# Products with the centroids in four column tiles, and one-hot rows moved by four copies

## The chip, the cores and the metric

The kernel runs on one core of a Trainium2 chip. A core has a matrix engine (TensorE, PE in the rows), a vector engine (VectorE, DVE), a scalar engine (ScalarE, ACT), GpSimd (POOL) and SyncE (SP), which here issues nearly all copies. The metric is device time in microseconds of one execution, lower is better; the time of a kernel is the median of its runs.

## The reference

Clustered attention, and behind it two layers of experts. In the attention a key is seen by a query only where both have the same nearest centroid.

```python
q_n = q / (np.linalg.norm(q, axis=-1, keepdims=True) + 1e-06)        # k_n, c_n likewise
q_assign = np.argmax(np.einsum('bhsd,hcd->bhsc', q_n, c_n), axis=-1)  # k_assign likewise
mask = q_assign[:, :, :, None] == k_assign[:, :, None, :]
scores = np.where(mask, scale * np.matmul(q, k.transpose(0, 1, 3, 2)), -1000000000.0)
attn = softmax(scores)
x = np.matmul(attn, v)      # then _moe_ref(x, ...) and _moe2_ref(x, ...), eight experts each
```

There are 2 x 8 heads of 768 positions and 64 columns, with 16 centroids for each head. All data are float32.

## The kernel before

The attention works on *pairs* of heads, eight of them (`pairs`, 0 to 7). The 128 partitions hold the 64 columns of two heads. For each pair the loop `for i in range(len(seq) + LAG + 1)` makes twelve *turns* (`sl` 0 to 11), one for each of six blocks of 128 queries and each head. In a turn stand, in this order for every engine:

- `scores`: TensorE writes `pss` (one block of queries against all keys) into one of two PSUM buffers. Its operands are two pairs of tiles: `x1`, `y1` (high and low halves of q and k) and `x2`, `y2`, which hold one more half product in partitions 0 to 63 and *one-hot rows* in partitions 64 to 79: the query's centroid, and 0 or -2^100 for the key's. That product is the mask.
- `softmax_max`: DVE takes the maximum, `nm`.
- `tr_p` of the block two turns back: TensorE transposes `pe` into `ppt`, ACT and DVE copy it out as `pt`.
- `attend` and `fin`, in some turns: TensorE's `av` in turns 0, 4, 6 and 10, `px` with the `norm` operations `ri`, `lp` and `x` on DVE in turns 1 and 7.
- one step of `prep` for the *next* pair (step 0 in turn 0, and so on; in pair 0 the steps begin at turn `P0` = 2), and loads of q, k and v for the pair after it (`LD`).
- `softmax_exp`: ACT's `pe`. The scores' PSUM buffer is free for the turn after next when it is done.

`ps_t` is a pool of three PSUM buffers, which `plog`, `plt`, `poh`, `ppt`, `px` and the small `pws` share.

The steps of `prep` work as follows. `part` splits q and k into high and low halves: `qh` and `kh` on ACT, `ql` on DVE, `kl` on POOL. `logits` multiplies q and k with the centroids (`plog`), for the first 384 positions and then for the other 384, and scales by the centroids' norms (`lt`). `logits_t` transposes `lt` (`plt`). `argmax` finds the nearest centroid (`mx`, `eq`; POOL multiplies `eq` by `rev`), `first` makes the one-hot `oh`. `operands` copies the halves into `x1`, `y1`, `x2`, `y2`: twelve copies on SP's queue, six for each head. `oh_t` transposes `oh` (`poh`), writes `ot` on DVE and copies its rows into `x2` and `y2`, each row of 16 partitions, four copies.

Every engine takes its instructions in the program's order, and SP's queue too: a copy that waits for its data holds up those behind it. In pair 6 the weights' pool takes over the memory of the preparation (`prepared.close()`) and the first weight piece is split there (`wh` on ACT, `wl` on DVE). Pairs 3, 4 and 5 carry in addition the routing of the first layer, many small operations on DVE.

Of the kernel before, what the change touches and what calls it, by code (L numbers as in the profile page):

```python
# [15 lines left out]
BIG = float(2.0 ** 100)  # L16
WARM = 8
P0 = 2
LD = {7: "q", 8: "k", 9: "v"}
WARM2 = 6  # L20


# [6 lines left out]
def attention(tc, end, ps_t, ident, wu, q, k, v, centroids, wg, x_half, lg_sb, consts, before_half, after_half, extra, slot):  # L29
# [13 lines left out]
    with ExitStack() as ctx:  # L43
# [11 lines left out]
        def cpy(dst, src):  # L55
            nc.sync.dma_start(dst.bitcast(F32), src.bitcast(F32))

        def centroid_norms():

            nc.vector.tensor_tensor(c_sq, cw, cw, op=ALU.mult)  # L60
            p = ps_t.tile([P, 512], F32, tag="t", name="pc")[:64, :NP]
            for hp in range(NP):
                for t in range(2):
                    nc.tensor.matmul(p[32 * t:32 * t + 2 * G, hp:hp + 1], c_sq[:, hp].rearrange("p j g -> p (j g)"),
                                     ones, start=True, stop=True)
            nc.scalar.sqrt(c_n, p)
            nc.vector.tensor_scalar_add(c_n, c_n, 1e-6)
            nc.vector.reciprocal(c_n, c_n)
# [17 lines left out]
        def gate_loads(wgv):  # L86
            for j in range(2):
# [2 lines left out]

        cw = one.tile([P, NP, 2, G], F32, name="cw")
        c_sq = one.tile([P, NP, 2, G], F32, name="c_sq")
        c_n = one.tile([64, NP], F32, name="c_n")
        ones = one.tile([P, 1], F32, name="a_ones")
        rev = one.tile([P, G], F32, name="rev")
        msc = one.tile([64, 2], F32, name="msc")
        rw = end.tile([P, NP, P + 2 * E], F32, name="rw")
        xs = {(nm, s, j): one.tile([P, S], F32R, name=f"{nm}_{s}{j}")
              for s in range(2) for j in range(2) for nm in ("x2", "y2")}

        warm0 = one.tile([1, 1], F32, name="warm0")
        st = {}
# [13 lines left out]
        def part(pi, nm):  # L116

            d = st[pi]
            t = d[nm] = w1.tile([P, S], F32R, tag=nm, name=nm)
            x = d[nm[0]]  # L120
            if nm == "qh":
                nc.scalar.activation(t, x, AF.Copy, scale=scale)
            elif nm == "ql":
                nc.vector.scalar_tensor_tensor(t, x, scale, d["qh"], op0=ALU.mult, op1=ALU.subtract)
            elif nm == "kh":
                nc.scalar.copy(t, x)
            else:
                nc.gpsimd.tensor_tensor(t, x, d["kh"], op=ALU.subtract)
# [15 lines left out]
            cpy(xs["y2", s, j][:D], d["kl"][r])  # L144

        def logits(pi):
            b, hp = pairs[pi]
            d = st[pi]
            d["lt"] = lt = w1.tile([64, S], F32, tag="lt", name="lt")
            for hf in range(2):  # L150
                p = ps_t.tile([P, 512], F32, tag="t", name="plog")[:64, :W]
                for t, nm in enumerate("qk"):
                    nc.tensor.matmul(p[32 * t:32 * t + 2 * G], cw[:, hp].rearrange("p j g -> p (j g)"),  # L153
                                     d[nm][:, hf * W:(hf + 1) * W], start=True, stop=True)
                if hf == 0:
                    nc.scalar.mul(lt[:, :W], p, c_n[:, hp:hp + 1])
                elif pi == 0:
                    nc.scalar.mul(lt[:, W:], p, c_n[:, hp:hp + 1])
                else:
                    nc.vector.tensor_scalar_mul(lt[:, W:], p, c_n[:, hp:hp + 1])  # L160

        def logits_t(pi):
            d = st[pi]
            p = ps_t.tile([P, 512], F32, tag="t", name="plt")[:, :C * 4 * G]
            d["lg"] = p.rearrange("p (c t j g) -> p c t j g", c=C, t=2, j=2)
            for c in range(C):
                nc.tensor.transpose(p[:, c * 4 * G:(c + 1) * 4 * G], d["lt"][:, c * P:(c + 1) * P], ident[:64, :64])
# [18 lines left out]

        def oh_t(pi):
            d = st[pi]
            ot = w1.tile([64, S], F32R, tag="lt", name="ot")
            ohv = d["oh"].rearrange("p (c i) g -> p c (i g)", i=4)  # L190
            for hf in range(2):
                p = ps_t.tile([P, 512], F32, tag="t", name="poh")[:64, :W]
                for c in range(HALF):
                    nc.tensor.transpose(p[:, c * P:(c + 1) * P], ohv[:, hf * HALF + c], ident)
                nc.vector.tensor_scalar(ot[:, hf * W:(hf + 1) * W], p, msc[:, 0:1], msc[:, 1:2],
                                        op0=ALU.mult, op1=ALU.add)
            s = pi % 2
            for j in range(2):
                cpy(xs["x2", s, j][64:64 + G], ot[j * G:(j + 1) * G])
                cpy(xs["y2", s, j][64:64 + G], ot[(2 + j) * G:(3 + j) * G])  # L200

        def first_mask(j):

# [142 lines left out]
        def last():  # L346
# [83 lines left out]
        for i in range(len(seq) + LAG + 1):  # L430
            cur = seq[i] if i < len(seq) else None
            if cur:
                scores(*cur)
                softmax_max(*cur)
            if LAG <= i < len(seq) + LAG:
                pi, c, j = seq[i - LAG]
                tr_p(pi, c, j)
                if j == 1 and c % HALF == HALF - 1:
                    hf = c // HALF
                    for w, at in enumerate(AT_LAST if pi == NPR - 1 else AT):  # L440
                        f = (lambda pi=pi, hf=hf, w=w: attend(pi, hf, w)) if w < 2 else (lambda pi=pi, hf=hf: fin(pi, hf))
                        if w < 2 or pi < NPR - 1 or hf == 0:
                            avq.append((i + at, f))
            while avq and (avq[0][0] <= i or i >= len(seq) + LAG - 1):
                avq.pop(0)[1]()
            if cur:
                pi = cur[0]
                sl = i % n
                if sl in LD:
                    load(pi + 2, LD[sl])  # L450
                if i == 0:
                    for _ in masks[1]:
                        pass
                if i == 1:
                    first_rows(1)
                ps = sl - P0 + (sl - P0 > 6) if pi == 0 else sl
                if pi + 1 < NPR and 0 <= ps < len(prep):
                    prep[ps](pi + 1)
                if pi >= 1 and sl % 2 == 0:
                    next(more, None)  # L460
                softmax_exp(*cur)
                if pi == NPR - 2 and sl == len(prep):
                    prepared.close()
                slot(pi, sl)
            if bg:
                bg.pop(0)()
# [1482 lines left out]
```

## Time and profile before

| | |
|---|---|
| median of 3 runs | 626.52 us (625.83 to 628.45) |
| the profiled execution | 623.46 us, span of its records 621.7 us |
| TensorE (PE) busy | 570.0 us, 92% of the span |
| VectorE (DVE) busy | 466.4 us, 75% |
| ScalarE (ACT) busy | 421.8 us, 68% |
| GpSimd (POOL) busy | 216.4 us, 35% |
| attention part | about 0 to 281 us, the experts from there |

Busy time of the matmul engine is modelled, since matmuls are pipelined; the distance from one instruction's start to the next one's start is the safer number. A timeline row gives the start and the length in us, the engine, the source line, the operation, the tiles (out<-in) and how often it follows itself; in brackets the idle time before it and what ended that.

### The profile page before, as it was taken

The page shows a single profiled execution, that of the slowest core. Times are in us where ns is not written, and L with a number is a line of the kernel's source. Part 1 is how long each engine was busy: PE and PEld are TensorE (multiplying, and loading weights), DVE is VectorE, ACT ScalarE, POOL GpSimd, SP SyncE. Part 2 cuts the span into 40 slices and gives each one's busy share as a digit, 9 for nine tenths or more (in the row PEclk, how much of TensorE's full clock was granted, in tenths as well). Part 3 has the DMA queues.
Part 4 walks back from the last instruction along what each step waited for, and adds up shares of the span by engine and source line. Part 5 has one row for each costly group of instructions (what it writes and reads, how often), then busy time and mean ns, then how long its engine had stood idle before and what let it go on. Part 6 is the DMA issues. An engine that isn't in the chain of part 4 may idle for free.

```text
span 621.7 us, 14524 instructions
## 1 busy us (share of the span) xinstructions
PE 570.0 (92%) x5428; PEld 467.1 (75%) x5428; DVE 466.4 (75%) x1185; ACT 421.8 (68%) x902; POOL 216.4 (35%) x427
## 2 busy tenths in 40 slices
PE   7899999998999998986799999997788999999993
PEld 2676767676767675656778998996777888999993
DVE  4776777677989676867577778789678566979881
ACT  3666666777676667963585687776774566979781
POOL 7702020201341110105743355636523723253541
PEclk9999999999999999999899999999999999999997
DMA  5589654656519891522456856976963677898930
GB/s 138 155 208 289 166 135 118 143 134 134 148 29 224 258 249 23 198 69 105 146 179 236 277 181 206 305 259 191 302 206 98 220 222 240 293 307 291 333 126 23
DMA packets 75518, 117.55 MB, mean 189 GB/s; under 512 B 10504, under 2 KB 43400, under 8 KB 75441
## 3 DMA queue, kind: packets, MB, share of 16 engines
q1 hardware_dynamic: 72017, 106.76, 57.4%
q0 software_dynamic: 3264, 9.72, 4.8%
q8 instruction: 45, 0.74, 0.5%
q14 instruction: 32, 0.26, 0.1%
q10 hardware_dynamic: 160, 0.07, 0.0%
HBM read 84.28 MB, written 12.87 MB: 156 GB/s over the span
## 4 chain that ended last, share of the span: by engine, by line
PE 61%; DVE 15%; ACT 11%; issue 4%; DMA 4%; POOL 2%; SPq 0%; ACTq 0%; DVEq 0%; POOLq 0%
PE ph L949 15%; PE py L1021 13%; PE av L280 9%; PE pss L238 8%; PE ppt L268 6%; PE pz L996 3%; DVE nm L246 3%; DVE wl L846 3%; ACT pe L254 2%; PE pyo L1637 2%; ACT wh L839 2%; ACT pt L270 1%; PE pxt L926 1%; PE plog L153 1%; DMA x2d<-xo 1%
## 5 line engine op out<-in xcount | busy, mean ns | idle before, releaser
L846 DVE SCALAR_TENSOR_TENSOR wl<-raw,sw,wh 128x1024 f16<-128x1024 f32 x128 | 163.6, 1285 | 19.0 <-ACT wh L839 18.8
L839 ACT ACTIVATE wh<-raw,sw 128x1024 f16<-128x1024 f32 x128 | 146.1, 1148 | 3.0 <-DMA x<-ot 2.5
L246 DVE TENSOR_REDUCE nm<-pss 128x1 f32<-128x768 f32 x96 | 91.4, 952 | 41.5 <-PE pss L238 37.8
L254 ACT ACTIVATE pe<-pss,nm 128x768 f32<-128x768 f32 x96 | 87.1, 907 | 24.3 <-DVE nm L246 24.3
L949 PEld LDWEIGHTS <-wh 128*128 128x128 f16 x1152 | 87.7, 99 | 17.4 <-issue 12.8
L238 PE MATMUL pss<-y,x 128*128 128x384 f32 x384 | 95.4, 370 | 4.0 <-ACT pe L254 3.2
L268 PE MATMUL ppt<-ident,pe 128*128 128x128 f32 x576 | 80.5, 275 | 3.3 <-ACT pt L270 1.4
L238 PEld LDWEIGHTS pss<-y,x 128*128 128x128 f32 x384 | 64.7, 194 | 24.6 <-issue 12.5
L270 ACT COPY pt<-ppt 128x384 f32<-128x384 f32 x128 | 57.9, 482 | 29.6 <-PE ppt L268 29.3
L949 PE MATMUL ph<-xh,wh 128*128 128x192 f16 (+14 forms) x576 | 67.3, 240 | 9.9 <-ACT hr L955 4.6
L268 PEld LDWEIGHTS ppt<-ident,pe 128*128 128x128 f32 x576 | 69.2, 142 | 8.9 <-ACT pt L270 2.3
L1021 PEld LDWEIGHTS <-wh 128*128 128x128 f16 x960 | 72.4, 99 | 4.3 <-issue 1.0
L280 PE MATMUL av<-pt,v 128*64 128x384 f32 x384 | 68.8, 494 | 0.0
L949 PE MATMUL ph<-xl,wh 128*128 128x192 f16 (+14 forms) x576 | 67.2, 240 | 0.4 <-DVE xl L928 0.3
L949 PE MATMUL ph<-xh,wl 128*128 128x192 f16 (+14 forms) x576 | 67.3, 240 | 0.0
L951 ACT ACTIVATE hh<-ph 128x128 f16<-128x128 f32 (+14 forms) x144 | 44.6, 316 | 25.9 <-PE ph L949 24.7
L958 DVE SCALAR_TENSOR_TENSOR hl<-ph,hh 128x192 f16<-128x192 f32 (+14 forms) x126 | 40.8, 335 | 26.1 <-ACT hh L951 25.9
L1021 PE MATMUL py<-hh,wh 128*128 128x192 f16 (+13 forms) x480 | 46.6, 239 | 1.5 <-ACT hh L951 1.0
L1021 PE MATMUL py<-hl,wh 128*128 128x192 f16 (+13 forms) x480 | 46.8, 239 | 0.5 <-DVE hl L958 0.2
L949 PEld LDWEIGHTS <-wl 128*128 128x128 f16 x576 | 45.5, 99 | 1.9
L280 PEld LDWEIGHTS av<-pt,v 128*64 128x64 f32 x384 | 24.8, 136 | 28.4 <-issue 28.3
L1021 PE MATMUL py<-hh,wl 128*128 128x192 f16 (+13 forms) x480 | 46.1, 239 | 0.0
(326 smaller groups left out, 873.4 us busy)
## 6 DMA issues: line engine op xcount, KB each, us to landing
raw<-in_moe_w SPq DMA_DIRECT2D x64, 1024.0 KB, 6.2
y<-kh SPq DMA_DIRECT2D x31, 192.0 KB, 4.0
x<-qh SPq DMA_DIRECT2D x30, 192.0 KB, 4.2
q<-in_q SPq DMA_DIRECT2D x8, 384.0 KB, 4.9
k<-in_k SPq DMA_DIRECT2D x8, 384.0 KB, 4.6
x<-ql SPq DMA_DIRECT2D x16, 192.0 KB, 3.5
v<-in_v SPq DMA_DIRECT2D x8, 384.0 KB, 3.3
out<-zt SPq DMA_DIRECT2D x1, 3072.0 KB, 11.3
```

The source lines that it names most:

```text
L238: nc.tensor.matmul(p[:, hf, :W], xx[:, c * P:(c + 1) * P], yy[:, hf * W:(hf + 1) * W], start=a, stop=o)
L246: nc.vector.tensor_reduce(nm, p[:, :, :W], axis=AX.XY, op=ALU.max, negate=True)
L254: nc.scalar.activation(pe, p[:, :, :W], AF.Exp, bias=d["nm", c, j], scale=1.0, accum_out=d["sm"][:, c, j:j + 1])
L268: nc.tensor.transpose(p[:, kc * P:(kc + 1) * P], pe[:, kh, kc * P:(kc + 1) * P], ident)
L270: eng(pt[:, kh * HALF:(kh + 1) * HALF, (c % HALF) * P:(c % HALF + 1) * P], p.rearrange("p (a b) -> p a b", a=HALF))
L280: nc.tensor.matmul(p[j * D:(j + 1) * D, :W], d["v"][:, j, kc, :], d["pt", hf, j][:, kc, :], start=(kc == 0), stop=(kc == C - 1))
L839: nc.scalar.activation(hi[:, :, s], x[:, :, s], AF.Copy, scale=sw)
L846: nc.vector.scalar_tensor_tensor(lo[:, :, s], x[:, :, s], sw, hi[:, :, s], op0=ALU.mult, op1=ALU.subtract, accum_out=fl)
L949: nc.tensor.matmul(p[:, :N], w[:, c, fs], x[:, c, :N], start=(k == 0), stop=(k == 11))
L951: nc.scalar.activation(hh[:, f, :N], p[:, :N], AF.Relu)
L958: nc.vector.scalar_tensor_tensor(hl[:, f, :N], p[:, :N], 0.0, hh[:, f, :N], op0=ALU.max, op1=ALU.subtract)
L1021: nc.tensor.matmul(p[:, :N], w[:, f, s], x[:, f, :N], start=(k == 0), stop=(k == 23))
```

## The change

- `logits` makes one round for both halves of the positions: four products, each with 32 output partitions (0, 32, 64, 96), in one PSUM buffer. `lt` is one tile of 128 partitions and 384 columns, written by one operation (DVE; ACT in pair 0's own).
- `logits_t` and `oh_t` make three transposes of 128x128 instead of six narrower ones.
- `ot` is made twice, once for each head, with the other head's rows scaled to zero (`msc`, which is now made from `own` on DVE and POOL at the start), so that the rows of both heads lie side by side and four copies of 32 partitions move them (before: four copies of 16 partitions, one for each head and each of x and y). `x2` and `y2` of both heads are one tile (`xs2`).
- `prep` has another order: `logits` in turn 0, `logits_t` and `qh` in 1, `argmax`, `kh` and `kl` in 2, `ql` in 3, `first` and `operands` in 4, `oh_t` in 7 (before: `qh` in 0, `ql`, `kh`, `kl` in 1, `logits` in 2, `logits_t` in 3, `argmax` and `operands` in 4, `first` in 5, `oh_t` in 8).
- The loads of q and k stand behind `oh_t` in turn 7, that of v in turn 8 (before: turns 7, 8 and 9). In pair 0 they move with the steps, to turns 9 and 10.

```diff
-LD = {7: "q", 8: "k", 9: "v"}
+LD = {7: "qk", 8: "v"}
...
-            d["lt"] = lt = w1.tile([64, S], F32, tag="lt", name="lt")
+            d["lt"] = lt = w1.tile([P, W], F32, tag="lt", name="lt")
+            p = ps_t.tile([P, 512], F32, tag="t", name="plog")[:, :W]
             for hf in range(2):
-                p = ps_t.tile([P, 512], F32, tag="t", name="plog")[:64, :W]
                 for t, nm in enumerate("qk"):
-                    nc.tensor.matmul(p[32 * t:32 * t + 2 * G], cw[:, hp].rearrange("p j g -> p (j g)"),
+                    r = 64 * hf + 32 * t
+                    nc.tensor.matmul(p[r:r + 2 * G], cw[:, hp].rearrange("p j g -> p (j g)"),
                                      d[nm][:, hf * W:(hf + 1) * W], start=True, stop=True)
-                if hf == 0:
-                    nc.scalar.mul(lt[:, :W], p, c_n[:, hp:hp + 1])
-                elif pi == 0:
-                    nc.scalar.mul(lt[:, W:], p, c_n[:, hp:hp + 1])
-                else:
-                    nc.vector.tensor_scalar_mul(lt[:, W:], p, c_n[:, hp:hp + 1])
+            if pi == 0:
+                nc.scalar.mul(lt, p, c_n[:, hp:hp + 1])
+            else:
+                nc.vector.tensor_scalar_mul(lt, p, c_n[:, hp:hp + 1])
...
-            for c in range(C):
-                nc.tensor.transpose(p[:, c * 4 * G:(c + 1) * 4 * G], d["lt"][:, c * P:(c + 1) * P], ident[:64, :64])
+            for c in range(HALF):
+                nc.tensor.transpose(p[:, c * P:(c + 1) * P], d["lt"][:, c * P:(c + 1) * P], ident)
...
-            ot = w1.tile([64, S], F32R, tag="lt", name="ot")
-            ohv = d["oh"].rearrange("p (c i) g -> p c (i g)", i=4)
+
+            ot = w1.tile([P, 2, W], F32R, tag="ot", name="ot")
+            ohv = d["oh"].rearrange("p (c i) g -> p c (i g)", i=8)
+            p = ps_t.tile([P, 512], F32, tag="t", name="poh")[:, :W]
+            for c in range(HALF):
+                nc.tensor.transpose(p[:, c * P:(c + 1) * P], ohv[:, c], ident)
+            for j in range(2):
+                nc.vector.tensor_scalar(ot[:, j], p, msc[:, j, 0:1], msc[:, j, 1:2], op0=ALU.mult, op1=ALU.add)
+            s = pi % 2
             for hf in range(2):
-                p = ps_t.tile([P, 512], F32, tag="t", name="poh")[:64, :W]
-                for c in range(HALF):
-                    nc.tensor.transpose(p[:, c * P:(c + 1) * P], ohv[:, hf * HALF + c], ident)
-                nc.vector.tensor_scalar(ot[:, hf * W:(hf + 1) * W], p, msc[:, 0:1], msc[:, 1:2],
-                                        op0=ALU.mult, op1=ALU.add)
-            s = pi % 2
-            for j in range(2):
-                cpy(xs["x2", s, j][64:64 + G], ot[j * G:(j + 1) * G])
-                cpy(xs["y2", s, j][64:64 + G], ot[(2 + j) * G:(3 + j) * G])
+                for t, nm in enumerate(("x2", "y2")):
+                    r = 64 * hf + 32 * t
+                    cpy(xs2[nm, s][64:96, :, hf * W:(hf + 1) * W], ot[r:r + 32])
...
         prep = [
-            lambda i: part(i, "qh"),
-            lambda i: (part(i, "ql"), part(i, "kh"), part(i, "kl")),
             lambda i: logits(i),
-            lambda i: logits_t(i),
-            lambda i: (argmax(i), operands(i, 0), operands(i, 1)),
-            lambda i: first(i),
+            lambda i: (logits_t(i), part(i, "qh")),
+            lambda i: (argmax(i), part(i, "kh"), part(i, "kl")),
+            lambda i: part(i, "ql"),
+            lambda i: (first(i), operands(i, 0), operands(i, 1)),
             lambda i: None,
             lambda i: None,
             lambda i: oh_t(i),
...
-                if sl in LD:
-                    load(pi + 2, LD[sl])
...
-                ps = sl - P0 + (sl - P0 > 6) if pi == 0 else sl
+                ps = sl - P0 if pi == 0 else sl
                 if pi + 1 < NPR and 0 <= ps < len(prep):
                     prep[ps](pi + 1)
+                for nm in LD.get(ps, ()):
+                    load(pi + 2, nm)
```

What this does to the order on VectorE in turns 1 to 4 of pair 1, from the `norm` operations' last, `x`, to the one-hot `oh`, was before:

```order
L323 TENSOR_TENSOR x<-px,ri 128x3x128
L124 SCALAR_TENSOR_TENSOR ql<-q,qh 128x768
L246 TENSOR_REDUCE nm<-pss 128x1
L270 COPY pt_762<-ppt 128x3x128
L160 TENSOR_SCALAR lt<-plog,c_n 64x384
L246 TENSOR_REDUCE nm<-pss 128x1
L270 COPY pt_791<-ppt 128x3x128
L246 TENSOR_REDUCE nm<-pss 128x1
L270 COPY pt_762<-ppt 128x3x128
L174 TENSOR_REDUCE mx<-plt 128x24
L176 TENSOR_TENSOR eq<-plt,mx 128x384
L246 TENSOR_REDUCE nm<-pss 128x1
```

The same stretch of VectorE in the changed kernel, with `lt` ahead of it in turn 0:

```order
L325 TENSOR_TENSOR x<-px,ri 128x3x128
L248 TENSOR_REDUCE nm<-pss 128x1
L272 COPY pt_764<-ppt 128x3x128
L175 TENSOR_REDUCE mx<-plt 128x24
L177 TENSOR_TENSOR eq<-plt,mx 128x384
L248 TENSOR_REDUCE nm<-pss 128x1
L272 COPY pt_793<-ppt 128x3x128
L124 SCALAR_TENSOR_TENSOR ql<-q,qh 128x768
L248 TENSOR_REDUCE nm<-pss 128x1
L272 COPY pt_764<-ppt 128x3x128
L184 TENSOR_REDUCE m_832<-eq 128x24
L186 TENSOR_TENSOR oh<-eq,m_832 128x384
```

`mx` and `eq` moved from turn 4 to turn 2, `ql` from turn 1 to turn 3, and the last two rows, `first`, from turn 5 to turn 4.

VectorE again, in turns 7 to 9 of pair 1, around `ot`, before:

```order
L323 TENSOR_TENSOR x<-px,ri 128x3x128
L246 TENSOR_REDUCE nm<-pss 128x1
L270 COPY pt_950<-ppt 128x3x128
L195 TENSOR_SCALAR ot<-poh,msc 64x384 x2
L1386 CAST cap<-cap_i 128x1
```

And in the changed kernel:

```order
L325 TENSOR_TENSOR x<-px,ri 128x3x128
L197 TENSOR_SCALAR ot<-poh,msc 128x384 x2
L248 TENSOR_REDUCE nm<-pss 128x1
L272 COPY pt_955<-ppt 128x3x128
L1395 CAST cap<-cap_i 128x1
```

`ot` moved ahead of turn 8's `nm`.

SyncE's queue at the end of pair 1's preparation of pair 2, from the last operand copy on (`x_` and `y_` with a number are here the tiles `x2` and `y2`), before:

```order
L56 DMA y_01_168<-kl 64x768
L114 DMA q<-in_q 128x768
L114 DMA k<-in_k 128x768
L56 DMA x_00_165<-ot 16x768
L56 DMA y_00_166<-ot 16x768
L56 DMA x_01_167<-ot 16x768
L56 DMA y_01_168<-ot 16x768
```

And in the changed kernel:

```order
L56 DMA y_0_166<-kl 64x768
L56 DMA x_0_165<-ot 32x2x384
L56 DMA y_0_166<-ot 32x2x384
L56 DMA x_0_165<-ot 32x2x384
L56 DMA y_0_166<-ot 32x2x384
L114 DMA q<-in_q 128x768
L114 DMA k<-in_k 128x768
```

The two loads moved behind the four copies.

## Rows read from the trace of the kernel before

**Rows 1.** Timeline of PE, pair 2 (start us, length us).
```profile
81.80 0.90 PE L307 MATMUL px<-rw,avo 128*128 128x144 f32 x6
82.61 0.97 PE L238 MATMUL pss<-y,x 128*128 128x384 f32 x4
...
84.17 0.51 PE L153 MATMUL plog<-q,cw 128*32 128x384 f32 x1
...
85.36 0.51 PE L153 MATMUL plog<-q,cw 128*32 128x384 f32 x1 [0.35 <-ACT pt L270]
...
86.15 0.95 PE L238 MATMUL pss<-y,x 128*128 128x384 f32 x4
...
89.75 2.16 PE L280 MATMUL av<-pt,v 128*64 128x384 f32 x12
...
92.15 0.97 PE L238 MATMUL pss<-y,x 128*128 128x384 f32 x4
...
93.53 0.96 PE L238 MATMUL pss<-y,x 128*128 128x384 f32 x4
...
100.71 0.92 PE L194 MATMUL poh<-ident,oh 128*64 128x128 f32 x6
```

**Rows 2.** Waits, 20 to 285 us (total us, times, longest).
```profile
PE plog L153 <- ACT pt L270: 3.6, 6, 1.4
...
ACT wh L839 <- DMA x<-ot: 2.5, 1, 2.5
...
PE pss L238 <- DMA y<-ot: 0.8, 1, 0.8
```

**Rows 3.** Costliest groups on the page (busy us, mean ns of one).
```profile
L246 DVE TENSOR_REDUCE nm<-pss 128x1 f32<-128x768 f32 x96 | 91.4, 952 | 41.5 <-PE pss L238 37.8
L254 ACT ACTIVATE pe<-pss,nm 128x768 f32<-128x768 f32 x96 | 87.1, 907 | 24.3 <-DVE nm L246 24.3
```

**Rows 4.** Windows: length, then busy us of each engine in pair 5.
```profile
180.00:200.00 20.00, 19.32 (x134) 13.51 (x132) 19.55 (x43) 12.82 (x28) 8.05 (x8) 1.00 0.61 151
```

**Rows 5.** Timeline of PE in the experts' part, four column tiles.
```profile
347.81 0.72 PE L1666 MATMUL pq<-yt,wgc 128*32 128x304 f32 x8
```

**Rows 6.** Timeline of DVE, pair 3.
```profile
122.47 0.55 DVE L174 TENSOR_REDUCE mx<-plt 128x24 f32<-128x384 f32 x1
123.05 0.56 DVE L176 TENSOR_TENSOR eq<-plt,mx 128x384 f32<-128x384 f32 x1
...
129.78 0.96 DVE L246 TENSOR_REDUCE nm<-pss 128x1 f32<-128x768 f32 x1 [1.67 <-PE pss L238]
...
131.86 0.96 DVE L246 TENSOR_REDUCE nm<-pss 128x1 f32<-128x768 f32 x1
...
133.20 1.25 DVE L195 TENSOR_SCALAR ot<-poh,msc 64x384 fp32r<-64x384 f32 x2
```

**Rows 7.** Timeline of ACT, pair 3, turn 1.
```profile
114.23 0.86 ACT L126 CAST kh<-k 128x768 fp32r<-128x768 f32 x1
```

**Rows 8.** Timelines of DVE and POOL: the first masks, and pair 2's argmax.
```profile
13.24 1.65 DVE L217 TENSOR_TENSOR oh<-eq,m 128x192 f32<-128x192 f32 x1
...
20.86 0.36 DVE L217 TENSOR_TENSOR oh<-eq,m 128x192 f32<-128x192 f32 x1
...
12.87 1.79 POOL L128 TENSOR_TENSOR kl<-k,kh 128x768 fp32r<-128x768 f32 x1
...
91.83 0.99 POOL L177 TENSOR_TENSOR eq<-eq,rev 128x384 f32<-128x384 f32 x1 [5.65 <-DVE eq L176]
```

**Rows 9.** Timeline of SP's queue, pair 0.
```profile
29.68 0.55 SPq L56 DMA_DIRECT2D x<-ql  x1
...
36.98 0.60 SPq L56 DMA_DIRECT2D y<-kl  x1
```

**Rows 10.** Copies issued, all of the span (KB each, median us to landing).
```profile
q<-in_q SPq DMA_DIRECT2D x8, 384.0 KB, 4.9
...
x<-ot SPq DMA_DIRECT2D x14, 48.0 KB, 2.3
```

More of the change, by code (lines that the diff above doesn't have):

```diff
@@ L60, in centroid_norms @@
             nc.vector.tensor_tensor(c_sq, cw, cw, op=ALU.mult)
-            p = ps_t.tile([P, 512], F32, tag="t", name="pc")[:64, :NP]
+            p = ps_t.tile([P, 512], F32, tag="t", name="pc")[:, :NP]
             for hp in range(NP):
-                for t in range(2):
+                for t in range(4):
                     nc.tensor.matmul(p[32 * t:32 * t + 2 * G, hp:hp + 1], c_sq[:, hp].rearrange("p j g -> p (j g)"),
@@ L92, in attention @@
         c_sq = one.tile([P, NP, 2, G], F32, name="c_sq")
-        c_n = one.tile([64, NP], F32, name="c_n")
+        c_n = one.tile([P, NP], F32, name="c_n")
         ones = one.tile([P, 1], F32, name="a_ones")
         rev = one.tile([P, G], F32, name="rev")
-        msc = one.tile([64, 2], F32, name="msc")
+        msc = one.tile([P, 2, 2], F32, name="msc")
         rw = end.tile([P, NP, P + 2 * E], F32, name="rw")
-        xs = {(nm, s, j): one.tile([P, S], F32R, name=f"{nm}_{s}{j}")
-              for s in range(2) for j in range(2) for nm in ("x2", "y2")}
+        xs2 = {(nm, s): one.tile([P, 2, S], F32R, name=f"{nm}_{s}") for s in range(2) for nm in ("x2", "y2")}
+        xs = {(nm, s, j): t[:, j] for (nm, s), t in xs2.items() for j in range(2)}
         warm0 = one.tile([1, 1], F32, name="warm0")
@@ L223, in first_rows @@
                     nc.tensor.transpose(p[:, c * P:(c + 1) * P],
-                                        oh0[j][:, hf * HALF + c].rearrange("p t g -> p (t g)"), ident)
+                                        oh0[j][:, 2 * c + hf].rearrange("p t g -> p (t g)"), ident)
                 hs = slice(hf * W, (hf + 1) * W)
@@ L378, in attention @@
             nc.gpsimd.memset(oh0[j], 0.0)
-        for (p0, c0, x) in ((0, 0, 1.0), (0, 1, 0.0), (32, 0, BIG), (32, 1, -BIG)):
-            nc.vector.memset(msc[p0:p0 + 32, c0:c0 + 1], x)
         keep_warm(WARM)
@@ L409, in attention @@
         zero_rows(1)
+        own = one.tile([P, 2], F32, name="own")
+        for j in range(2):
+            nc.vector.tensor_reduce(own[:, j:j + 1], ident.rearrange("p (a i g) -> p a i g", i=2, g=G)[:, :, j],
+                                    axis=AX.XY, op=ALU.add)
+        for p0 in (0, 64):
+            nc.gpsimd.memset(msc[p0:p0 + 32, :, 0:1], 1.0)
+            nc.gpsimd.memset(msc[p0:p0 + 32, :, 1:2], 0.0)
+            nc.gpsimd.tensor_scalar(msc[p0 + 32:p0 + 64, :, 0], own[p0 + 32:p0 + 64], BIG, None, op0=ALU.mult)
+            nc.gpsimd.tensor_scalar(msc[p0 + 32:p0 + 64, :, 1], own[p0 + 32:p0 + 64], -BIG, None, op0=ALU.mult)
         consts()
```

## Prediction

> **What bounds the kernel now.** I first read the attention part, where the change lies: eight pairs of heads, twelve turns each, and in each turn TensorE does scores (`pss`), transposes (`ppt`) and whatever else stands there. [rows 1] shows the pace. A plain turn of TensorE takes 93.53 - 92.15 = 1.38 us from one `pss` to the next. The turn with the products with the centroids takes 86.15 - 82.61 = 3.54, 2.16 more, of which 0.35 is a wait for a PSUM buffer that ACT frees. Such waits sum to 3.6 us over six pairs, the longest 1.4 [rows 2]. So TensorE sets the pace wherever a turn holds extra TensorE work. A plain turn has little to spare, though: its scores become usable two turns later only after DVE's `nm` (952 ns) and ACT's `pe` (907 ns) [rows 3], 1.9 us in a row, and `pss` two turns on needs that PSUM buffer back. Two plain turns are 2.76 us, so DVE may be about 0.8 us late and no more. In 180 to 200 us DVE is itself busy for 19.55 of 20 us [rows 4]; there TensorE's savings buy nothing. Two stalls go back to the one-hot copies: `wh` waits 2.5 us for `x<-ot`, `pss` 0.8 us for `y<-ot` [rows 2].
>
> **What each part takes off TensorE.** (1) `plog`. Now: two rounds of two column tiles and a buffer wait, 2.16 us. Afterwards one round: TensorE reaches the first product 84.17 - 82.61 = 1.56 us after `pss` and needs 86.15 - 85.36 = 0.79 from the last round's start to the next `pss`, so the turn is 2.35 and the extra 0.97. Saved: 1.19. This needs four column tiles to run at once; the trace has such a case, `pq`: eight records of 304 columns, two for each of four tiles, within 0.72 us [rows 5]. At 304 columns, against 384 for `plog`, that scales to 0.91 at most, fixed part included. Between 0.79 and 0.91 I take 0.79, since `plog`'s own round has the same columns.
> The Trainium skill (TensorE: Matmul & The Clock Gate, Measured speedup vs the span model) gives 2.38 times for three column tiles, less than three. By that share a round would be 0.79 / 0.79 = 1.0 us and the seven pairs would lose 1.5 us of what is saved; the `pq` row is of four tiles in this kernel, and it decides.
> (2) `plt` and `poh`: six narrow transposes each become three full ones. Six for `poh` take 0.92 us [rows 1]; I take half of that less the pipeline's fill, 0.4, and 0.25 for `plt`, which has half the columns. Together 1.85 us a pair on TensorE. ACT also loses one `lt`, DVE none: its one `lt` has twice the partitions and the same columns.
>
> **What the new order costs.** Now take an undisturbed pair and count from the `pss` of turn 2. Before, turn 2 held `plog` and turn 3 `plt`; now both are plain for TensorE (2 x 1.38), but DVE has `argmax` in turn 2 and `ql` in turn 3. `pss` is 0.97 long, so `nm` starts at 1.07. `nm` and `pt` take 133.20 - 131.86 = 1.34, `mx` 0.58, `eq` 0.56 [rows 6]: the next `nm` starts at 3.55 and `ql` could at 4.89. ACT has `kh` (0.86, [rows 7]) in front of turn 2's `pe`: the first half of `ppt` is through at about 1.35 (estimate), `pt` and `kh` end about 2.5, `pe` at 3.4. TensorE wants that buffer at 2 x 1.38 = 2.76: **stall 0.7**.
> Then the port. `oh` has two SBUF inputs and takes 0.36 us alone; at 13.24 it took 1.65, until `kl` on POOL (12.87 + 1.79 = 14.66) was through [rows 8]. One of the two waits for the other's end. In the old order `ql` stood before `kl`, so POOL waited and nobody with it. Now `kl` stands directly behind POOL's `eq` (0.99, [rows 8]): DVE's `eq` ends at 1.07 + 1.34 + 0.58 + 0.56 = 3.55, POOL's at about 4.6, `kl` runs 4.6 to 6.4. `ql` comes at 4.9, waits to 6.4 and ends at 7.2. Behind it on DVE stands turn 4's `nm`, so its `pe` ends at about 9.2; TensorE (3.4, then a turn with `av` of 1.38 + 2.16 [rows 1], then a plain one) wants that buffer at 8.3 to 8.4: **stall 0.8**. It is a close race: `kl` comes first by 0.3 us.
> In turn 7 `ot` now stands behind the `norm` operations and in front of turn 8's `nm`. From one `nm` to the next with `norm` between are 131.86 - 129.78 = 2.08; `ot` adds 1.25 [rows 6]: turn 8's `nm` starts at 1.07 + 2.08 + 1.2 = 4.3, its `pe` ends at 6.3. TensorE's turn 7 is a plain one with `px` (82.61 - 81.80 = 0.81, [rows 1]) and half a `poh`, 0.4, so some 2.5, and it wants turn 10 at 2.5 + 2 x 1.38 = 5.3: **stall 1.0**. Before, `ot` stood behind that `nm`, and the turn with `av` covered what it delayed.
> Sum for an undisturbed pair: -1.85 + 0.7 + 0.8 + 1.0 = some **+0.6 us**. The whole saving is given back. The bounds are -1.85 (no stall at all) and +1.3 (all stalls, and no saving but the 1.19 of `plog`).
>
> **Pair by pair.** *Pair 0 with the way in.* `plog` and the first mask come some 1 us earlier, and the first `oh`, now at about 12.3, gets in front of `kl` and takes 0.36 instead of 1.65: -1.9 when the scores begin. Against it: `ql` moves two turns back and then waits for `kl`; counting DVE's queue on from the first scores in the same way, it ends at about 33.5 us (estimate). The nine copies from `x<-ql` to `y<-kl` went at 29.68 to 36.98 and 0.6 [rows 9]; they are bound by their bytes, so now they end near 42, and the four copies from `ot` behind them near 44.4. An idle queue lands them 2.3 us later [rows 10], a full one in 3 to 4. The first `pss` of pair 1 needs the last of them, at 46.5 to 48, where TensorE, by the same count, would be there at about 45. I take 1.9 lost: **0** (from -1.9 to +1.5).
> *Pairs 1 and 2*: 2 x 0.6 = **+1.2**. *Pair 3*: its `plog` waits some 0.5 longer than the 0.35 of [rows 1], and that goes: **+0.1**. *Pair 4* holds the longest such wait (1.4): 0.6 - 1.0 = **-0.4**. *Pair 5* is bound by DVE: **0**. *Into pair 6*: the 0.8 us for `y<-ot` goes, as the copies stand in front of two loads: **-0.8**. *Pair 6*: `wh`'s wait was 2.5 us, of which TensorE felt about 1.7; copies one turn earlier, in a turn that `av` covers, remove it: 0.6 - 1.7 = **-1.1**. *Pair 7* prepares nothing, and what follows just starts earlier.
> Sum: 0 + 1.2 + 0.1 - 0.4 + 0 - 0.8 - 1.1 = -1.0 us. The profiled execution took 623.46 (span 621.7), so 622.5 in its terms; it is 3 us faster than the median of the runs, 626.52, which becomes **625.5**.
>
> **Rivals.** *A. TensorE is the bound throughout*: no stall appears. Six pairs save 1.85 each, pairs 3 and 4 another 1.5, the way in 1.9, the two stalls 2.5: -17, 609.5. For it: TensorE has few waits before. Against: the two-turn chain above, and [rows 4].
> *B. `ql` gets to the port first.* Then `kl` waits and nobody with it: 0.8 less in pairs 1, 2, 3 and 6, and pair 0 keeps its 1.9: -1.0 - 3.2 - 1.9 = -6.1, **620.4**. For it: only 0.3 us part the two. Against: DVE comes later wherever it has more to do. The Trainium skill (SBUF — State Buffer, Who interferes with whom) says that whoever issues first holds the shared pair for a whole instruction; the `oh` row agrees, 1.65 against 0.36.
> *C. Slower: `q` and `k` land too late.* They are now sent behind the four copies from `ot` and land 4.9 us after [rows 10]; `plog`, which needs both, is now in turn 0 and no longer in turn 2, and TensorE stands still with it. In an undisturbed pair they are sent some 7 to 7.5 us after turn 7's `pss` and land by 12.4, `plog` comes at 14.7: no wait. It decides where the copies are more than 2.3 us late, as in pair 0 and where DVE is late (pairs 4 and 5). At 1.5 us for each of three, -1.0 + 4.5 = +3.5: **630**.
>
> **How the numbers follow.** About 0.5% (3.1 us) is what a measurement here can tell from no change. Forecast 0.45, A 0.08, B 0.27, C 0.20. Faster: A, B and the lower edge of the forecast, 0.39; slower: C, 0.20; same: 0.41. The forecast's own range is 622.5 to 628.5 (each of the three stalls 0.2 us more or less, in five pairs). The range that leaves out A and the worse half of C is 619 to 629.5.
>
> **What would show it.** Right: four `plog` records starting together and no wait for ACT among them; `pss` of turns 4, 6 and 10 waiting for ACT's `pe`; `ql` at 2 us or more with `kl` beside it; the waits for `x<-ot` and `y<-ot` of [rows 2] gone; pairs 1 and 2 as long as before or longer; the first scores 2 us earlier. Wrong: `ql` at 0.95 us with a long `kl` (B), turns 2 and 3 at 1.38 (A), `plog` waiting for a load (C). Most easily wrong are the copies into pair 1 and the pairs with routing work on DVE, which I have not laid out turn by turn.

## The result, and the profile after

The changed kernel takes 628.82 us (median of 20 runs, 626.09 to 631.71), the kernel before 625.43 beside it (20 runs, 619.31 to 628.56). The ratio is 1.006, 95% interval 1.0039 to 1.0082: slower by 2.4 to 5.1 us. The forecast was 625.5 and 1 us faster. The profiled execution takes 627.75 us, span 625.9.

The chain of the steps on TensorE is read best from where each pair's first `pss` starts (us, from the timelines of TensorE; "last" is turn 11 of pair 7):

| | pair 0 | 1 | 2 | 3 | 4 | 5 | 6 | 7 | last | span |
|---|---|---|---|---|---|---|---|---|---|---|
| before | 16.14 | 45.98 | 76.71 | 107.76 | 139.54 | 173.15 | 205.08 | 238.79 | 269.54 | 621.7 |
| changed | 13.40 | 41.85 | 73.57 | 104.69 | 135.58 | 168.74 | 201.28 | 238.96 | 271.05 | 625.9 |
| difference | -2.7 | -4.1 | -3.1 | -3.1 | -4.0 | -4.4 | -3.8 | +0.2 | +1.5 | +4.2 |

From pair 1 to pair 6 the changed kernel is 3.1 to 4.4 us ahead. It loses all of that, and more, within the last turns of pair 6; a rest of 2.7 us comes behind the attention.

First what went as forecast. Timeline of PE, pair 2 after, against [rows 1]:

```profile
77.17 0.51 PE L155 MATMUL plog<-q,cw 128*32 128x384 f32 x1
77.18 0.51 PE L155 MATMUL plog<-k,cw 128*32 128x384 f32 x1
77.19 0.51 PE L155 MATMUL plog<-q,cw 128*32 128x384 f32 x1
77.19 0.51 PE L155 MATMUL plog<-k,cw 128*32 128x384 f32 x1
...
77.96 0.96 PE L240 MATMUL pss<-y,x 128*128 128x384 f32 x4
```

The products of all four column tiles begin within 0.02 us, and from the first of them to the next `pss` are 77.96 - 77.17 = 0.79 us, as forecast.

The three stalls, in pair 1 (timelines of PE, then of DVE, then of POOL):

```profile
50.91 0.97 PE L240 MATMUL pss<-y,x 128*128 128x384 f32 x4
52.94 0.97 PE L240 MATMUL pss<-y,x 128*128 128x384 f32 x4 [0.39 <-ACT pe L256]
56.58 0.97 PE L240 MATMUL pss<-y,x 128*128 128x384 f32 x4
58.70 0.96 PE L240 MATMUL pss<-y,x 128*128 128x384 f32 x4 [0.49 <-ACT pe L256]
...
66.12 0.94 PE L240 MATMUL pss<-y,x 128*128 128x384 f32 x4
68.55 0.97 PE L240 MATMUL pss<-y,x 128*128 128x384 f32 x4 [0.83 <-ACT pe L256]
```

```profile
54.25 2.50 DVE L124 SCALAR_TENSOR_TENSOR ql<-q,qh 128x768 fp32r<-128x768 f32 x1
```

```profile
54.11 1.82 POOL L128 TENSOR_TENSOR kl<-k,kh 128x768 fp32r<-128x768 f32 x1
```

Against a plain turn of 1.38 us, the turns that end with the `pss` of turns 4, 6 and 10 take 2.03, 2.12 and 2.43: stalls of 0.65, 0.74 and 1.05, forecast 0.7, 0.8 and 1.0. (The brackets hold only the idle time that the modelled ends leave; the whole loss is in the distance of the starts.) `kl` came to the port 0.14 us before `ql`, which then took 2.50 us.

Now the loss. Waits, 20 to 285 us (total us, times, longest), against [rows 2]:

```profile
PE pss L240 <- ACT pe L256: 17.8, 17, 6.6
...
ACT wh L848 <- DMA x<-ot: 8.1, 1, 8.1
...
PEld plog L155 <- DMA k<-in_k: 0.9, 1, 0.9
...
PE pss L240 <- DMA y<-ot: 0.5, 1, 0.5
```

`wh`, the first weight piece, waits 8.1 us for the one-hot copies and no longer 2.5. The loads of q and k, rival C, cost one wait of 0.9 us. The place itself in three timelines, of SP's queue, ACT and PE:

```profile
221.53 0.94 SPq L56 DMA_DIRECT2D y<-kl  x1
222.67 2.01 SPq L821 DMA_DIRECT2D raw<-in_moe_w  x2
225.22 2.24 SPq L56 DMA_DIRECT2D x<-ot  x1
...
229.54 0.60 SPq L56 DMA_DIRECT2D y<-ot  x1
```

```profile
236.49 1.15 ACT L848 ACTIVATE wh<-raw,sw 128x1024 f16<-128x1024 f32 x1 [8.08 <-DMA x<-ot]
...
237.91 0.90 ACT L256 ACTIVATE pe<-pss,nm 128x768 f32<-128x768 f32 x1
```

```profile
230.78 0.97 PE L240 MATMUL pss<-y,x 128*128 128x384 f32 x4
...
238.96 1.65 PE L240 MATMUL pss<-y,x 128*128 128x384 f32 x4 [6.55 <-ACT pe L256]
...
243.98 0.96 PE L240 MATMUL pss<-y,x 128*128 128x384 f32 x4
```

The same place in the kernel before, SP's queue, ACT and PE:

```profile
222.44 1.98 SPq L812 DMA_DIRECT2D raw<-in_moe_w  x2
232.01 0.56 SPq L56 DMA_DIRECT2D x<-ot  x1
...
236.33 1.15 ACT L839 ACTIVATE wh<-raw,sw 128x1024 f16<-128x1024 f32 x1 [2.45 <-DMA x<-ot]
...
238.79 0.97 PE L238 MATMUL pss<-y,x 128*128 128x384 f32 x4 [1.72 <-ACT pe L254]
```

In the changed kernel two weight loads of 1 MB (`raw`) stand in SP's queue directly ahead of the four one-hot copies. The copies are issued from 225.22 us, 6.8 us earlier than in the kernel before (232.01), and yet `wh` starts at 236.49, where it started at 236.33 before: what it needs lands at the same time. Before, the loads went out at the same time, 222.44 to 224.42, but the copies 7.6 us behind them. `pe` of turn 10 stands behind `wh` on ACT, and `pss` of turn 12 (pair 7's first) needs that buffer: TensorE stands still for 6.55 us. Then it runs slowly: that `pss` takes 1.65 us and not 0.97, and the turn 5.02 and not 3.64. Windows of the changed kernel (length, busy PE, PEld, DVE, ACT, POOL; then granted clock, DMA share, GB/s):

```profile
224.00:232.00 8.00, 7.17 (x48) 5.30 (x47) 5.42 (x10) 2.85 (x7) 1.49 (x2) 1.00 1.00 310
232.00:236.00 4.00, 0.40 (x4) 0.16 (x2) 1.28 (x2) 0.00 (x0) 0.00 (x0) 0.90 0.51 107
236.00:244.00 8.00, 5.04 (x23) 3.29 (x23) 2.25 (x3) 5.67 (x10) 0.00 (x0) 0.62 0.00 0
```

The DMA engines are full to 232 us (share 1.00), and the granted clock is 0.62 in the 8 us behind the stop: mostly the lower of its two levels, 1.2 GHz of 2.4.

Of the rest behind the attention a part comes with a lower clock. The same stretch of the experts' part in three kernels (one window each; before, changed, and the kernel of the second experiment, whose experts' part is that of before):

```profile
420.00:440.00 20.00, 15.78 (x204) 14.66 (x203) 18.78 (x65) 13.59 (x32) 12.09 (x23) 1.00 0.68 219
```

```profile
420.00:440.00 20.00, 17.25 (x189) 16.07 (x187) 18.35 (x63) 12.51 (x28) 11.24 (x23) 0.83 0.59 190
```

```profile
420.00:440.00 20.00, 16.99 (x208) 15.59 (x206) 18.84 (x60) 13.64 (x30) 12.82 (x22) 0.91 0.73 229
```

The clock falls there in the changed kernel (0.83) and not in the one profiled execution of before (1.00), but it falls in the third too (0.91). Weight pieces that came 1.95 us late at 410 to 430 us come 3.5 us late from 454 us on.

### The profile page after: what moved, and what is told of

Read it like the earlier page. It is cut to its first block, busy times and chain, and to the rows that moved or that the text cites. A ratio compares the mean times of both kernels' runs of the same rounds, so it can differ in the third digit from the quotient of the medians.

```text
span 625.9 us, 14440 instructions
## 1 busy us (share of the span) xinstructions
PE 561.4 (90%) x5399; PEld 463.6 (74%) x5399; DVE 470.6 (75%) x1183; ACT 416.9 (67%) x894; POOL 220.9 (35%) x435
## 4 chain that ended last, share of the span: by engine, by line
PE 60%; DVE 17%; ACT 11%; issue 6%; DMA 3%; POOL 2%; SPq 0%; ACTq 0%; DVEq 0%; POOLq 0%
PE ph L958 15%; PE py L1030 12%; PE av L282 9%; PE pss L240 8%; PE ppt L270 5%; DVE nm L248 4%; PE pz L1005 3%; ACT pe L256 3%; DVE wl L855 3%; PE pyo L1646 2%; ACT wh L848 2%; PE pxt L935 1%; DVE ql L124 1%; PE plog L155 1%; DMA k<-in_k 1%
## 5 line engine op out<-in xcount | busy, mean ns | idle before, releaser
L240 PE MATMUL pss<-y,x 128*128 128x384 f32 x384 | 93.0, 363 | 18.8 <-ACT pe L256 17.8
L240 PEld LDWEIGHTS pss<-y,x 128*128 128x128 f32 x384 | 62.7, 190 | 39.7 <-ACT pe L256 24.3
```

The costliest lines, as they stand in the source:

```text
L240: nc.tensor.matmul(p[:, hf, :W], xx[:, c * P:(c + 1) * P], yy[:, hf * W:(hf + 1) * W], start=a, stop=o)
```

## Experiments

Theory Q: the loss is the landing of the one-hot copies behind 2 MB of weights. Rival O: the new order's stalls are the loss. Each ratio is to the kernel before on the same chip. The times in the expectations were written with 625.4 us for the kernel before; beside the runs it takes 621.8, 625.1 or 622.7, so expectation and result are compared by their ratios.

**1. Weight loads behind the copies** (`raw_behind`, changed kernel).

```diff
-         (-2, 4): ('load',),
-         (-2, 6): ('load',),
+         (-2, 7): ('load', 'load'),
```

> Changed kernel, with the last two of the four early 1 MB weight loads moved in pair 6 from turns 4 and 6 to turn 7, so that they stand behind the four one-hot copies in SP's queue and no longer ahead of them. Theory Q (the loss is the first weight piece `wh`, which waits 8.1 us at 228 to 236 us for the one-hot copies, and those land late because 2 MB of weights stand ahead of them): the copies, issued from about 225 us, land by 230; `wh` waits under 2 us, TensorE's 6.55 us gap falls under 1, the half-speed `pss` after it goes, the last `pss` comes 6 to 8 us earlier, and the time is 619 to 622. Rival O (the new order's stalls of 0.4 to 0.8 us in turns 4, 6 and 10 are the loss, and the gap only moves time that TensorE would wait anyway): `wh` may wait less, but the time stays at 627 to 629. Rival W (`wh` waits for the weights' own transfers or for the bandwidth of all of it, not for what stands ahead in the queue): the wait stays at 6 us or more, 627 to 630.

Measured: ratio 0.996 (0.9932 to 0.9988), 618.02 us against 621.83. Timelines of SP's queue, ACT and PE:

```profile
225.27 0.68 SPq L56 DMA_DIRECT2D x<-ot  x1
...
227.38 0.60 SPq L56 DMA_DIRECT2D y<-ot  x1
228.18 1.22 SPq L821 DMA_DIRECT2D raw<-in_moe_w  x2
```

```profile
230.75 1.15 ACT L848 ACTIVATE wh<-raw,sw 128x1024 f16<-128x1024 f32 x1 [2.29 <-DMA x<-ot]
```

```profile
230.82 0.97 PE L240 MATMUL pss<-y,x 128*128 128x384 f32 x4
233.21 0.97 PE L240 MATMUL pss<-y,x 128*128 128x384 f32 x4 [0.76 <-ACT pe L256]
236.85 0.97 PE L240 MATMUL pss<-y,x 128*128 128x384 f32 x4
```

From pair 1 to 230.8 us it runs within 0.2 us of the changed kernel, all stalls included. The copies go out from the same moment (225.27); `wh` starts 5.7 us earlier, the gap is 0.76, the `pss` behind it runs at full length, and the last `pss` comes at 263.94 instead of 271.05. From 1.006 to 0.996: Q holds. Rivals O and W both asked for 627 or more, a ratio of 1.0025, and O is not what made the kernel slower than before. Q missed a little: `wh` waits 2.29 us and not under 2, and 0.996 stands for 623 us and not 622.

**2. The same in the kernel before** (`before_raw_behind`: the two loads from turns 4 and 6 to turn 8).

> Kernel before, with the same two loads moved from turns 4 and 6 of pair 6 to turn 8, behind its one-hot copies. There the copies are issued at 232 us, after the loads have been taken up, and land 2.3 us after their issue, as in all other pairs. Theory Q: nothing to gain from the queue, `wh` waits 2 to 2.5 us as before, 624.5 to 626.5. Rival W (bandwidth): the wait of 2.5 us goes, 623 to 624.

Measured: 0.9992 (0.9961 to 1.0022); `wh` waits 2.4 us. In the old order the loads had been taken up before the copies came, and nothing hangs on where they stand. The interval alone would let rival W stand (623 to 624 us are 0.996 to 0.998); the wait, which did not go, decides against it. That copies land 2.3 us after their issue "in all other pairs" is not so: the last copies for pair 6, issued at 202.93 us behind the loads of q and k, were waited for until 206.48.

**3. The cause put into the kernel before** (`before_raw_between`).

```diff
-         (-2, 4): ('load',),
-         (-2, 6): ('load',),
+         (-2, 'mid'): ('load', 'load'),
...
                 cpy(xs["y2", s, j][64:64 + G], ot[(2 + j) * G:(3 + j) * G])
+                if j == 0 and pi == len(pairs) - 1:
+                    slot(pi - 1, 'mid')
```

> Kernel before, with the last two early 1 MB weight loads put between the first two and the last two one-hot copies of pair 6's preparation (before they stood ahead of the operand copies' end, long taken up when the one-hot copies were issued). This puts the suspected cause, 2 MB ahead of one-hot copies in the queue, into the kernel that does not have it. Theory Q: the last two copies land 4 to 6 us later, `wh` waits 6 to 8 us instead of 2.5, and the time is 3 to 6 us longer: ratio 1.005 to 1.010. Rival (the changed kernel's long wait comes from something else in it: doubled bytes of the copies, the freed memory): the wait stays near 2.5, ratio 0.998 to 1.002.

Measured: 1.0132 (1.0089 to 1.0175). Timelines of ACT and PE:

```profile
242.21 1.15 ACT L841 ACTIVATE wh<-raw,sw 128x1024 f16<-128x1024 f32 x1 [9.57 <-DMA x<-ot]
```

```profile
244.67 1.65 PE L240 MATMUL pss<-y,x 128*128 128x384 f32 x4 [8.83 <-ACT pe L256]
```

The same kind of wait, and the same slow `pss`, with none of the change in the kernel. It is dearer than expected: the wait is 7.1 us longer than before and not 3.5 to 5.5, and the turn behind it takes 5.94 us instead of 3.64, which the expectation had not counted. The Trainium skill (DMA: Bandwidth & Descriptors, Two DMAs through the same engine are not ordered) says that within one queue of one engine descriptors start in order; this run (9.57 us of wait with the loads in front of the last two copies) and the first (2.29 with the loads behind all four) agree.

**4. The piece later, the loads where they were** (`piece_later`, changed kernel).

```diff
-         (-2, 9): ('open_ring', 'open_first', 'piece'),
+         (-2, 9): ('open_ring', 'open_first'),
          (-2, 10): ('gather',),
          (-2, 11): ('piece',),
+         (-1, 0): ('piece',),
```

> Changed kernel, with the first weight piece two turns later (turn 11 of pair 6 instead of 9; the next in turn 0 of pair 7 instead of turn 11), and the loads where they were. Theory Q: ACT has no `wh` in front of turn 9's `pe`; the copies still land at about 236, `wh` comes at about 237 and waits under 1 us, TensorE's gap is under 1 us or is replaced by a wait of `pss` for the copies themselves in turn 0 of pair 7 (it would be there at about 233.5): then 2.5 us of wait instead of 6.55. Time 621 to 625. Rival O: 627 to 629.

Measured: 1.0018 (0.9992 to 1.0044). Timeline of PE:

```profile
232.32 0.60 PE L240 MATMUL pss<-y,x 128*128 128x384 f32 x2
236.19 1.14 PE L240 MATMUL pss<-y,x 128*128 128x384 f32 x2 [3.28 <-DMA x<-ot]
241.25 0.97 PE L240 MATMUL pss<-y,x 128*128 128x384 f32 x4
```

Without `wh` in the way, TensorE comes to pair 7 at 232.32 and waits for the one-hot rows themselves, up to 236.19. So it is the copies that are late, and `wh` only made their lateness felt sooner. The time gained less than Q expected (621 to 625 us are 0.993 to 0.999): the wait is 3.28 us and not 2.5, and the rest of its turn is slow, 5.06 us from 236.19 to 241.25. By its time alone this run does not tell Q from O; the trace does.

**5. The products without the new order** (`old_order`: the steps and loads in the order of before, products and copies of the change).

> The parts apart: the changed kernel's products, transposes and copies (four column tiles, three wide transposes, four copies of 32 partitions), with the order of the steps and the loads of the kernel before. Theory Q with the prediction's prices: TensorE saves up to 1.85 us a pair where DVE leaves room, no stall of the new order, and the first weight piece waits about as in the kernel before (2 to 3 us, since in the old order the copies come a turn later, when the loads have been taken up): 615 to 621. Rival O expects the same size of gain, 7 us or more, and for the reason that the stalls are gone; what tells Q from O is this run beside the one with the loads moved. Rival P (the products in four column tiles save nothing, or the doubled copy bytes cost it again): 625 to 629.

Measured: 1.0013 (0.998 to 1.0045): nothing gained, against what both theories expected, and the time that rival P expected. But P's first reason is not it. Pair 2 takes 29.70 us (before 31.05, changed 31.12), so the products do save where no copy is waited for. In pair 1 the turns with `plog`, `plt` and `poh` take 2.38, 1.71 and 1.70 instead of 3.51, 2.07 and 2.13: 1.92 us, forecast 1.85. But now TensorE comes to the copies before they have landed. Timelines of PE (into pair 1, into pair 6) and ACT:

```profile
43.34 0.88 PE L240 MATMUL pss<-y,x 128*128 128x384 f32 x2 [1.54 <-DMA x<-ot]
```

```profile
200.99 0.41 PE L240 MATMUL pss<-y,x 128*128 128x384 f32 x1 [1.56 <-DMA y<-ot]
```

```profile
232.48 1.15 ACT L849 ACTIVATE wh<-raw,sw 128x1024 f16<-128x1024 f32 x1 [3.44 <-DMA x<-ot]
```

The first turns of pairs 1 and 6 take 7.33 and 7.57 us, 3.6 in a plain pair: the waits, and behind each a granted clock of 0.79 over 8 us. In this order the loads of q and k stand directly ahead of the copies in the queue (for pair 6 the loads go out from 192.61 us, the copies from 194.55, and the last one is waited for until 201.75). The early copies of the change, ahead of those loads, are the cover against this. How much of the waits is P's other reason, the doubled bytes, is not shown: the median from issue to landing is 3.0 us for `x<-ot` and 2.2 for `y<-ot` here, 2.3 and 2.1 in the kernel before.

**6. Only the early copies of the new order** (`old_steps_copies_7`: run 1 with the steps up to `first` as before, `oh_t` in turn 7 and the loads behind it).

> Changed kernel with the two weight loads behind the one-hot copies (as in the run raw_behind) and the steps up to `first` in the order of the kernel before; `oh_t` and with it the copies stay in turn 7, in front of the loads of q and k. So of the new order only the early copies are left. If the new order's stalls are what the prediction says (it puts 0.7 on turn 4 and 0.8 on turn 6, the changed kernel's trace shows 0.4 and 0.5 to 0.8), those two go, and pairs 1 to 6 get 0.5 to 1.4 us shorter each than in raw_behind: 2 to 5 us less, ratio to the kernel before 0.988 to 0.993. Rival L (once TensorE is earlier, the landing of the copies takes over, as in old_order, whose `pss` waited 1.5 us for the one-hot copies at pair 1 and again at pair 6): nothing gained on raw_behind, 0.995 to 0.998, with waits for x<-ot or y<-ot of 1 us and more.

Measured: 0.9903 (0.9866 to 0.9941, 6 runs). The last `pss` comes at 260.95, 3.0 us before that of run 1; the stalls of turns 4 and 6 are gone, that of turn 10 is there (0.83).

**7. `kl` ahead of `eq`** (`kl_first`, on top of run 1).

```diff
-            lambda i: (argmax(i), part(i, "kh"), part(i, "kl")),
+            lambda i: (part(i, "kh"), part(i, "kl"), argmax(i)),
```

> raw_behind with `kl` ahead of `eq` on POOL (kh and kl stand before argmax in turn 2), so that `kl` is over when DVE comes to `ql`. The prediction's step: `ql` took 2.44 us and not 0.95 because `kl` held the port, and turn 6's `pss` waited for that. Then `ql` takes 0.95 in pairs 1, 2, 3 and 6, turn 6's wait of 0.43 to 0.54 goes, and the time falls by 1.5 to 3 us: ratio 0.991 to 0.994. Rival: another operation with two SBUF inputs on DVE (`oh`, or the operations of routing) meets `kl` or `eq` instead, or the turns are not bound there: 0.995 to 0.998.

Measured: 0.9927 (0.9897 to 0.9958); last `pss` at 261.57, 2.4 us before run 1. Timelines of DVE and POOL, pair 1:

```profile
53.22 1.42 DVE L124 SCALAR_TENSOR_TENSOR ql<-q,qh 128x768 fp32r<-128x768 f32 x1
```

```profile
51.04 1.82 POOL L128 TENSOR_TENSOR kl<-k,kh 128x768 fp32r<-128x768 f32 x1 [2.07 <-ACT kh L126]
52.83 1.00 POOL L178 TENSOR_TENSOR eq<-eq,rev 128x384 f32<-128x384 f32 x1
```

`ql` waits now for POOL's `eq`, which is the shorter operation: 1.42 us instead of 2.50, though not 0.95 as expected, and the turn before turn 6 of pair 1 is plain (1.38). Of the 2.4 us 0.5 are there when the scores begin (12.62 us, 13.13 in run 1), which is within the scatter of the way in. The intervals of runs 1 and 7 overlap; the gain is read from the traces.

**8. Copies one turn later** (`copies_8`: run 1 with `oh_t` and the loads in turn 8, v in 9).

> raw_behind with `oh_t`, its copies and the loads behind them one turn later (turn 8 instead of 7, v in 9, weight loads in 8). The prediction's step: `ot` ahead of turn 8's `nm` makes turn 10's `pss` wait (1.0 forecast, 0.83 in the trace), one turn later it stands behind that `nm`, in front of turn 9's, and the `av` of turn 10 covers it: 0.4 to 0.8 us a pair less in pairs 1, 2, 3 and 6. Against it the copies go out 1.4 to 2.4 us later: the first `pss` of pair 1 waits 1 to 2 us more and `wh` 1 to 2 us more. Sum: ratio 0.993 to 0.997 if the stall is worth more than the lateness; 0.997 to 1.002 if the copies' landing decides.

Measured: 1.0004 (0.9977 to 1.003). Turn 10's stall goes (turns 8 and 9 of pair 1 take 1.70 and 1.41 instead of 1.35 and 2.43), and pair 1 pays for it. Timeline of PE:

```profile
41.58 0.60 PE L240 MATMUL pss<-y,x 128*128 128x384 f32 x2
44.89 0.41 PE L240 MATMUL pss<-y,x 128*128 128x384 f32 x1 [2.71 <-DMA y<-ot]
46.05 0.69 PE L240 MATMUL pss<-y,x 128*128 128x384 f32 x1 [0.75 <-DMA y<-ot]
```

Pair 1's first turn takes 11.32 us, 5.16 in run 1: the wait, and behind it a turn at low clock (0.59 from 44 to 52 us). Pair 7's first `pss` waits 2.26 us instead of 0.76, and its turn takes 5.09 us instead of 3.64.

**9. The first piece in turn 10** (`piece_10`, on top of run 6).

```diff
-         (-2, 9): ('open_ring', 'open_first', 'piece'),
-         (-2, 10): ('gather',),
+         (-2, 9): ('open_ring', 'open_first'),
+         (-2, 10): ('piece', 'gather'),
```

> old_steps_copies_7 with the first weight piece in turn 10 of pair 6 instead of turn 9, behind that turn's `pe`. There `wh` waited 2.4 us and the first `pss` of pair 7 0.90 for the `pe` behind it. In turn 10 the copies have landed when ACT comes to `wh` (under 0.5 us of wait), and `av` stands between: the 0.90 goes or falls under 0.3, and the time is 0.5 to 1 us shorter, ratio 0.986 to 0.992. Rival: the next `pe` is late in its place, or the piece makes the second one collide in turn 11: 0.990 to 0.995. With it the clock: should the granted clock fall again at 420 to 450 us, as in most runs of this study, the ratio is 0.990 and above whatever the attention does.

Measured: 613.17 us against 622.66, ratio 0.9868 (0.9823 to 0.9913, 6 runs): the lowest ratio here, ahead of both kernels. Its interval overlaps that of run 6; of the 2.55 us by which the last `pss` comes earlier (258.40) 1.0 lie at this place, as expected, and most of the rest in pairs 0 and 4, where the two do the same. Timelines of ACT and PE:

```profile
226.32 1.15 ACT L848 ACTIVATE wh<-raw,sw 128x1024 f16<-128x1024 f32 x1 [0.65 <-DMA x<-ot]
```

```profile
226.25 0.97 PE L240 MATMUL pss<-y,x 128*128 128x384 f32 x4
227.63 0.94 PE L240 MATMUL pss<-y,x 128*128 128x384 f32 x4
```

`wh` waits 0.65 us, a little more than expected, and pair 7 begins without a wait, at 227.63.

## Why the prediction was wrong

By its own terms, from the starts of `pss` (the 0.8 us that pair 1's first turn takes more than pair 2's are put to pair 0, whose copies it waits for):

| term | forecast | measured |
|---|---|---|
| way in | -1.9 | -2.7 |
| pair 0, copies into pair 1 | +1.9 | -0.6 |
| pairs 1 and 2 | +1.2 | +0.3 |
| pair 3 | +0.1 | -0.9 |
| pair 4 | -0.4 | -0.45 |
| pair 5 | 0 | +0.6 |
| into pair 6 | -0.8 | -1.0 |
| pair 6 | -1.1 | +6.4 |
| behind the attention | 0 | +2.7 |

**The step that failed is pair 6**: "copies one turn earlier, in a turn that `av` covers, remove it: 0.6 - 1.7 = -1.1". The wait of `wh` did not go; it grew from 2.5 to 8.1 us. TensorE lost 5.0 us up to pair 7 beyond what the pair took before (without the wait for `y<-ot`, counted above it), and 1.4 in the slow turn behind the stop. The step looked at when the copies are issued and gave no time to their landing; what the prediction has for it elsewhere are the 2.3 us of [rows 10], the median of all copies, and 3 to 4 for a full queue. It did not look at what stands ahead of them in the queue at that place: in pair 6 alone weight loads go out as well, two of them in turns 4 and 6. Yet for "into pair 6", one term earlier, the prediction had counted on just this: it took the wait for `y<-ot` away because the copies then stand in front of two loads. In the old order the weight loads had been taken up before the copies came. In the new one the operand copies wait for `ql`, the loads for the operand copies, and the one-hot copies for both. Runs 1 and 3 show this cause from both sides, run 4 that the copies are what is late.

**Right in mechanism and size**: the products (1.92 us against 1.85 in the old order, run 5), `kl` before `ql` at the port, and the three stalls (0.65, 0.74 and 1.05 against 0.7, 0.8 and 1.0). Run 6 takes the first two stalls away with the order of the steps, run 7 the second with the order on POOL, run 8 the third with the place of `ot`. The Trainium skill (TensorE: Matmul & The Clock Gate, Measured speedup vs the span model) would have had `plog` save less, by its 2.38 for three column tiles; the round took 0.79 us, not 1.0, and the measurement decides. **Right in sign, too dear**: an undisturbed pair was to lose 0.6. Pair 1, its wait for the copies left out, lost 0.2: the stalls sum to 2.44 us (forecast 2.5), but in their new turns `plog`, `plt` and `poh` add 0.77, 0.17 and 0.33 us where they added 2.13, 0.69 and 0.75, so 2.3 us are saved and not 1.85. Pair 2 lost 0.07 and is no plain pair: small operations for the weights (`pws`) stand in its turns 2 and 3, its stalls are 0.50 and 0.89 us there, and none before turn 6.

**Wrong on the other side**: pair 0. `ql` was to end at 33.5 us and the copies to land at 46.5 to 48; `ql` ended at 30.84, and pair 1's last wait for a copy ended at 43.13. TensorE did come early, at 41.85, and felt 0.5 us of it. Run 8 shows that a loss was near: copies one turn later cost 6.2 us in that turn. Together with the way in this is 3.3 us of gain that the sum gave away, and it hid part of pair 6's loss. That 628.8 us lie so near the forecast of 625.5 is luck: pair 6 and what lies behind the attention came out 10.2 us dearer than the sum, everything else 4.9 us cheaper. Rival C's 630 is near as well, but of its waits for q and k only one came, of 0.9 us.

**Behind the attention** the forecast had nothing. Of the 2.7 us some 1.6 come where the granted clock is 0.57, at 429 to 437 us, and right behind. In the profiles this came and went among kernels whose work there is the same, so it is not shown to belong to the change; what part of the 2.4 to 5.1 us is clock of this kind stays open. A sign that it is small: run 1, which has the change and no long stop, has a median granted clock of 0.983 over its executions, the kernel before beside it 0.985, and 0.002 of 618 us is about 1 us (estimate).

Of the way in, 0.9 us are scatter: the first scores begin at 15.20 to 16.14 us in the three profiles with the old way in, at 12.51 to 13.51 in those with the new. Pair 5 stays bound by DVE, as forecast (19.52 of 20 us busy from 180 to 200 us, 19.55 in [rows 4]); the 0.6 it lost was not tried.

## What to carry to other kernels

A copy that moves earlier lands earlier only if the queue ahead of it is empty then: read, at that very place, the bytes between it and the last landed transfer, and not the median of all copies of its name. An engine that gains some microseconds by cheaper work runs into the next transfer that was hidden: look for every wait on a landing that is short or zero and ask what it becomes when its waiter is 4 us earlier. Small copies that someone waits for belong ahead of large prefetches that nobody needs for many turns; here that order of the queue, of the new order the early copies alone, and the first piece one turn later turned +0.6% into -1.3%.

## What the runs showed of the hardware

A long stop of TensorE costs twice. After a wait of 6.55 us the granted clock was 0.62 over 8 us, after 3.28 us (run 4) it was 0.79 in the same window, and after 0.76 (run 1) it stayed at 1.00 from 228 to 244 us. The turn behind the longest took 5.02 us where 3.64 is plain, and in run 4 what was left of the turn took 5.06. The length of the last wait alone does not settle it: in the kernel before, a wait of 1.72 us (238.79) left the clock at 1.00 from 236 to 244 us; in run 5, one of 1.54 us (43.34) was followed by 0.79 from 42 to 50 us.
